# Max tiles of two neighbouring phases shared out by the number of filler matmuls in each

## The chip, the core and the metric

The kernel runs on one core of one Trainium2 chip. The core has a matrix engine (PE, whose weight loads are listed apart as PEld), a vector engine (DVE), a scalar engine for activations (ACT), a general engine (POOL) and a queue that issues transfers (SP). Each engine works through its own list of instructions in order and waits for the others on semaphores. The metric is the time of the core in device microseconds (us), lower is better; a kernel is run several times and the median counts.

## What is computed

The inputs are a matrix `x` of 2048 tokens by 640 channels and weights. The output mixes two branches with a gate per token.

```python
def _A_ref(x, wq, wk, wv, wo):          # 32 heads of 20 channels, one shared k and v
    q = (x @ wq).reshape(B, S, H, Dh).transpose(0, 2, 1, 3)
    k = x @ wk
    v = x @ wv
    scores = jnp.einsum("bhqd,bkd->bhqk", q, k) * (Dh ** -0.5)
    p = softmax(scores)
    o = jnp.einsum("bhqk,bkd->bhqd", p, v)
    return o.transpose(0, 2, 1, 3).reshape(B, S, H * Dh) @ wo

def _B_ref(x, w1, b1, w2, b2):          # an MLP over the token axis
    h = layernorm(x)
    u = gelu(jnp.einsum("bsd,sf->bdf", h, w1) + b1)     # F = 1728
    return (jnp.einsum("bdf,fs->bds", u, w2) + b2).transpose(0, 2, 1)

g = sigmoid((x * gate_w).sum(-1, keepdims=True))
out = g * _A_ref(...) + (1 - g) * _B_ref(...)
```

All is float32. Where a product needs the accuracy, the kernel splits a factor in a high and a low part and adds three products.

## The kernel before

**Stages.** A first stage (L147 to L380) projects `q`, `k`, `v` and normalizes `x`. A second stage (L499 to L532) does the first 10 of 28 groups of the MLP's first layer. Then comes the main loop (L906), 513 passes long, with which the change deals. A short piece (L943 to L957) ends the kernel.

**A phase.** One pass `k` of the main loop is called a phase here. Its number modulo 2 is `b`. The matrix engine is used as two row halves of 64 rows each, which stream side by side: half 0 has rows 0 to 63, half 1 has rows 64 to 127. In phase `k`, half `b` is the own half and half `1-b` is the filler half. A phase issues four kinds of matmuls:

- *Scores* (`qk`, L568): four matmuls of 62 x 512 on the own half, two for unit `k-1` and two for unit `k`. Each writes a bank of the pool `ps_s` (three buffers), and ACT turns it into `p` with an exponential (L578).
- *Max tiles* (`ms_next`, L398): matmuls of 60 x 512 on either half. They form the same scores ahead of time, only to find each row's maximum. Each writes a bank of the pool `ps_m` (three buffers) at L410, and DVE reduces it to one number per row (L413). There are 2048 of them. Within a pair of phases four are taken on each half.
- *Fillers*: matmuls of 64 x 320 on the filler half, which do the MLP's first layer (L828), its second layer (L668) or the output projection (L776), by the stage. They add up in one bank, `ps_g` (one buffer). Since the two halves take turns in adding to that bank, `signal` (L586) lets DVE write a small `flag` (L588) after the last filler of a phase, and the first filler of the next phase waits for that flag (`other_tile`, L581).
- *The product with v* (`pv_mm`, L596): at the end of each phase, with all 128 rows and in column tiles of 32. It adds unit `k-1` to the output `o`. Its four pieces need four `p` tiles, two of them from this phase's first two scores.

**The order in a phase.** L910 to L920 write the order out by hand. `lane_x` (L891) puts the own half's scores and max tiles in turns, a max tile first while there are any. `lane_f` (L898) puts the fillers of the other half, then `signal`, then that half's max tiles. `beside` (L880) merges the two lists by their running times, with `X_US` = 0.232 for a score or max tile and `F_US` = 0.147 for a filler (L878). It keeps the last item of the own half until the other list is empty:

```python
            if k == x and len(lanes[k]) == 1 and lanes[1 - k]:
                k = 1 - k
```

The result is one list for the matrix engine, and the reduces stand on DVE's list in the order of their max tiles, with `flag` where `signal` fell.

**How many fillers.** `batches` (L837) cuts each group of fillers into phases, and `ph` (L873) holds them. By its integer division the pairs of an even and the next odd phase have these fillers:

- first layer of the MLP, 90 pairs: 36 with (9, 9) and 54 with (10, 10);
- between the layers, 2 pairs with (0, 0), phases 180 to 183;
- second layer, 128 pairs, in turns (9, 10), (10, 11), (10, 10), (10, 11), phases 184 to 439;
- output projection, 24 pairs: 8 with (7, 7), 8 with (8, 8) in turns, phases 440 to 471, then 8 with (15, 15), phases 472 to 487;
- phase 488 (`k_tail`, L851) and after: no max tiles are left, and their fillers come from another list.

L910 gives the max tiles: three to the own half and one to the filler half where a phase has fewer than 12 fillers, else four and none.

**Work of DVE beside the max tiles.** Once in 16 phases `pv_mm` finishes an output group: DVE transposes it (L611), takes a reciprocal (L614) and, two phases later, transposes back (L618). These stand behind the reduces of the phase after which they are issued. The back transpose is issued after phases whose number is 3 modulo 16.

Of the kernel before, what the change touches and what calls it, by code (L numbers as in the profile page):

```python
# [37 lines left out]
def mix_kernel(ctx: ExitStack, tc: tile.TileContext, A_x, A_wq, A_wk, A_wv, A_wo,  # L38
               B_x, B_w1, B_b1, B_w2, B_b2, gate_w, out):
    nc = tc.nc  # L40
    x = A_x[0]
# [94 lines left out]
    def new_qmax(n):  # L136
        if n < NU and n not in qmax:
            qmax[n] = load_q(n, "qmx")
# [259 lines left out]
    def ms_next(b):  # L398
        k = given[b]
        if k >= 32 * NU:  # L400
            return None
        given[b] += 1
        n, r = divmod(k, 32)
        (kq, pr), qt = divmod(r // 4, 2), r % 4

        def step():
            if n not in mtiles:
                mtiles[n] = mpool.tile([P, 16, 4], F32, name="mp")
            ms = ps_m.tile([P, NB], F32, name="ms")
            nc.tensor.matmul(ms, qmax[n][64 * b:64 * b + 60, pr, qt * P:(qt + 1) * P],  # L410
                             kst[64 * b:64 * b + 60, kq * NB:(kq + 1) * NB], start=True, stop=True)
            c = (2 * b + pr) * 4 + qt
            nc.vector.tensor_reduce(mtiles[n][:, c, kq:kq + 1], ms, axis=AX.X, op=ALU.max)  # L413
            issued[b] += 1
            if min(issued) == 32 * n + 1:
                new_qmax(n + 1)

        return step

    def ms_done():  # L420
        n = len(row_max)
        if n < NU and min(issued) >= 32 * (n + 1):
            mm = mmpool.tile([P, 16], F32, name="mm")
            nc.vector.tensor_reduce(mm, mtiles.pop(n), axis=AX.X, op=ALU.max)
            mn = mmpool.tile([P, 2, 16], F32R, name="mn")
            nc.gpsimd.tensor_scalar(mm, mm, -1.0, None, op0=ALU.mult)
            nc.gpsimd.tensor_copy(mn[:, 0, :], mm)
            nc.gpsimd.tensor_sub(mn[:, 1, :], mm, f32(mn[:, 0, :]))
            row_max[n] = mn

    def store_max(n):
        mn = row_max[n]
        mt = mpool.tile([P, 32], F32, name="mt")
        nc.vector.transpose(mt, f32(mn).rearrange("p j c -> p (j c)"))
        nc.sync.dma_start(out=m_scr[n], in_=mt)

    def fetch_max(n):
        src = m_scr[n].rearrange("(i j b r) e -> j b r i e", j=2, b=2, r=8)
        for b in range(2):
            for j in range(2):  # L440
                rows = f32(qtiles[n][64 * b + 60 + j:64 * b + 61 + j])
                nc.sync.dma_start(out=rows.rearrange("o p (t i e) -> o (p t) i e", i=4, e=32), in_=src[j, b][None])
# [51 lines left out]
    def pop_chain():  # L494
        f = chain.pop(0) if chain else None
        if f:
            f()
# [70 lines left out]
    def qk(u, pr, b):  # L568
        n, kb = units[u]
        if kb == 4 and pr == 0 and b == 0:  # L570
            new_q(n + 1)
        q = qtiles[n]
        odd_s[0] ^= 1
        s = ps_m.tile([P, NB], F32, name="ms") if spare[0] and odd_s[0] and not loaded else ps_s.tile([P, NB], F32, name="s")
        nc.tensor.matmul(s, kst[64 * b:64 * b + 62, kb * P:(kb + 1) * P], q[64 * b:64 * b + 62, pr, :],  # L575
                         start=True, stop=True)
        p = pp_pool.tile([P, NB], F32, name="p")
        nc.scalar.activation(p, s, AF.Exp, scale=SCALE)  # L578
        ptiles[u, 2 * pr + b] = p
# [127 lines left out]
    def tail_load(i):  # L707
        if i < len(jobs):
            st, r0, r1 = jobs[i]
            cols = slice(st * P, (st + 1) * P)  # L710
            oT, yt = room(i)
            c0, c1 = r0 // P, r1 // P
            for j in range(2):
                nc.sync.dma_start(out=f32(oT[:, j, c0:c1]),
                                  in_=o_scr[j, r0:c1 * P, cols].rearrange("(c p) s -> p c s", p=P))
                if r1 > c1 * P:
                    nc.sync.dma_start(out=f32(oT[:r1 - c1 * P, j, c1]), in_=o_scr[j, c1 * P:r1, cols])
            if r0 == 0:
                nc.sync.dma_start(out=yt, in_=y_scr[cols, :])
            loaded.append(i)  # L720
# [31 lines left out]
    def tail_take(h, n):  # L752
        out = []
        while len(out) < n and tail[h] and tail[h][0][0] in loaded:
            out.append(tail[h].pop(0)[1])
        return out
# [43 lines left out]
    def last_wo():  # L800
        raw = fin.tile([P, D], F32, name="yo")
        nc.gpsimd.memset(raw, 0.0)
        for hh in range(4):
            r = (H - 4 + hh) * DH
            nc.sync.dma_start(out=raw[32 * hh:32 * hh + DH, :], in_=A_wo[r:r + DH, :])
        return raw

    def split_last(raw):
        hi, lo = spare_row(0, F32R), spare_row(1, F32R)
        nc.gpsimd.tensor_copy(hi, raw)  # L810
        nc.gpsimd.tensor_sub(lo, raw, f32(hi))
        return hi, lo
# [38 lines left out]
    k_tail = len(units) - TAIL  # L851
    todo = [divmod(i, FC) for i in range(PRO, 2 * FC)]
    seq = batches([b1_jobs(*t) for t in todo], [5] * len(todo))
    for i, (steps, rest, done) in enumerate(seq):
        item, j = divmod(i + 1, 5)
# [17 lines left out]
    ph = [(rows[1 - b], rest if b else [], done if b else []) for rows, rest, done in seq for b in range(2)]  # L873
# [3 lines left out]

    X_US, F_US = 0.232, 0.147  # L878

    def beside(rows0, rows64, x):  # L880
        lanes = [list(rows0), list(rows64)]
        at = [0.0, 0.0]
        while lanes[0] or lanes[1]:
            k = 0 if lanes[0] and (not lanes[1] or at[0] <= at[1]) else 1
            if k == x and len(lanes[k]) == 1 and lanes[1 - k]:
                k = 1 - k
            us, f = lanes[k].pop(0)
            f()
            at[k] += us

    def lane_x(ss, ms):  # L891
        out = []
        for x in ss:
            out += [(X_US, y) for y in ms[:1]] + [(X_US, x)]
            ms = ms[1:]
        return out + [(X_US, y) for y in ms]

    def lane_f(ms, fs, end):  # L898
        return [(F_US, f) for f in fs] + [(0.0, f) for f in [signal] + end] + [(X_US, y) for y in ms]
# [4 lines left out]
    with tc.manual_schedule(engines={mybir.EngineType.PE, mybir.EngineType.DVE, mybir.EngineType.Activation,  # L904
                                     mybir.EngineType.Pool, mybir.EngineType.SP}):
        for k in range(len(units) + 1):  # L906
            b = k % 2
            ss = [lambda u=u, pr=pr: qk(u, pr, b) for u in (k - 1, k) for pr in range(2) if 0 <= u < len(units)]
            fs, rest, done = ph[k] if k < k_tail else ([], [], [])
            ms = [[f for f in (ms_next(x) for _ in range(c)) if f] for x, c in (((b, 3), (1 - b, 1)) if len(fs) < 12 else ((b, 4), (1 - b, 0)))]  # L910
            lanes = [None, None]
            lanes[b] = lane_x(ss, ms[0])
            if k >= k_tail:
                rate = [len(t) / max(1, len(units) - k) for t in tail]
                own = tail_take(b, max(0, math.ceil(rate[b] - 2 * X_US / F_US)))
                lanes[b] = [x for i, y in enumerate(lanes[b])
                            for x in [y] + [(F_US, f) for f in own[len(own) * i // len(lanes[b]):len(own) * (i + 1) // len(lanes[b])]]]
                fs = tail_take(1 - b, math.ceil(rate[1 - b] + 2 * X_US / F_US))
            lanes[1 - b] = lane_f(ms[1], fs, done)
            beside(*lanes, b)  # L920
            ms_done()
            spare[0] = len(row_max) == NU
            for _ in range(2 if spare[0] else 1):
                f = later.pop(0) if later else None
                if f:
                    f()
            pop_chain()
            for f in rest:
                f()
            if k == k_tail - 4:  # L930
                raw = last_wo()
            if k == k_tail - 2:
                w_last = split_last(raw)
            if 13 <= k - k_tail < 17:
                tail_load(8 + k - k_tail - 13)
            if k:
                pv_mm(k - 1)
                n, kb = units[k - 1]
                if kb == 7 and n + 1 < NU:
                    store_max(n + 1)  # L940
                if kb == 9 and n + 1 < NU:
                    fetch_max(n + 1)
# [36 lines left out]
```

## Time and profile before

| quantity | value |
|---|---|
| median of 3 runs | 1727.07 us (1726.58 to 1728.19) |
| the profiled execution's own time | 1729.04 us |
| its span, first to last instruction | 1727.2 us |
| matrix engine busy | 1707.6 us, 99% of the span |
| DVE busy | 1450.4 us, 84% |
| ACT busy | 1187.3 us, 69% |
| POOL busy | 567.9 us, 33% |
| DMA, moved | 133.86 MB, mean 77 GB/s |
| mean granted matrix clock | 0.997 |

The profiled execution is one of its own, 1.84 us longer than its span and 1.97 us longer than the median of the other runs. Busy time of the matrix engine counts the two halves as one, so 99% does not tell that both halves are full. A row of the timeline gives the start and the length of an instruction or of several equal ones in a row (x and a number), and in brackets how long the engine had been idle before and what ended it. A weight load (PEld) that waits is the place where a matmul waits.

### The profile page before, as it was taken

The page shows a single profiled execution, that of the slowest core. Times are in us where ns is not written, and L with a number is a line of the kernel's source. Part 1 is how long each engine was busy: PE and PEld are TensorE (multiplying, and loading weights), DVE is VectorE, ACT ScalarE, POOL GpSimd, SP SyncE. Part 2 cuts the span into 40 slices and gives each one's busy share as a digit, 9 for nine tenths or more (in the row PEclk, how much of TensorE's full clock was granted, in tenths as well). Part 3 has the DMA queues.
Part 4 walks back from the last instruction along what each step waited for, and adds up shares of the span by engine and source line. Part 5 has one row for each costly group of instructions (what it writes and reads, how often), then busy time and mean ns, then how long its engine had stood idle before and what let it go on. Part 6 is the DMA issues. An engine that isn't in the chain of part 4 may idle for free.

```text
span 1727.2 us, 38831 instructions
## 1 busy us (share of the span) xinstructions
PE 1707.6 (99%) x14877; PEld 1110.6 (64%) x14877; DVE 1450.4 (84%) x2936; ACT 1187.3 (69%) x2313; POOL 567.9 (33%) x677
## 2 busy tenths in 40 slices
PE   9999999999999999999999999999999999999998
PEld 6889766666666666566666666666666666556665
DVE  6669988888888888888888888888888888888724
ACT  3434577777777777777777777777777777777764
POOL 5547644454444454332122222211222111111200
PEclk9999999999999999999999999999999999999999
DMA  6665312222222222112222222121122122244411
GB/s 200 194 162 130 103 53 59 69 58 75 63 70 69 69 63 51 47 47 68 61 68 67 58 61 61 55 57 49 46 57 61 53 61 63 74 138 131 143 52 36
DMA packets 164573, 133.86 MB, mean 77 GB/s; under 512 B 27639, under 2 KB 129428, under 8 KB 164388
## 3 DMA queue, kind: packets, MB, share of 16 engines
q1 hardware_dynamic: 164388, 131.39, 27.2%
q8 instruction: 117, 1.92, 0.5%
q14 instruction: 68, 0.56, 0.1%
HBM read 98.69 MB, written 31.65 MB: 75 GB/s over the span
## 4 chain that ended last, share of the span: by engine, by line
PE 95%; DVE 3%; DMA 1%; SPq 0%; ACT 0%; issue 0%; DVEq 0%; ACTq 0%
PE o L602 30%; PE s L575 17%; PE ms L410 17%; PE g L668 11%; PE g L828 8%; PE pp L261 4%; PE g L776 2%; PE pu L517 2%; PE ms L733 2%; DVE mp L413 2%; PE g L733 0%; DMA wr<-in_B_w_dram 0%; SPq L159 0%; DMA ht<-in_A_wq_dram 0%; PE pt L253 0%; DMA q_scr<-ql 0%
## 5 line engine op out<-in xcount | busy, mean ns | idle before, releaser
L413 DVE TENSOR_REDUCE mp<-ms 128x1 f32<-128x512 f32 x2048 | 1278.2, 684 | 173.3 <-PE ms L410 169.5
L578 ACT ACTIVATE p<-s 128x512 f32<-128x512 f32 x2048 | 1070.3, 602 | 412.0 <-PE s L575 406.2
L410 PE MATMUL ms<-kst,qmx 60*128 60x512 f32 x2048 | 847.7, 421 | 8.3 <-DVE mp L413 7.5
L575 PE MATMUL s<-qst,kst 62*128 62x512 f32 x2048 | 750.9, 403 | 0.1
L602 PE MATMUL o<-p,v_sb 128*32 128x512 f32 x4096 | 558.9, 605 | 0.5 <-ACT p L578 0.5
L410 PEld LDWEIGHTS ms<-kst,qmx 60*128 60x128 f32 x2048 | 379.0, 185 | 225.6 <-DVE flag L588 180.3
L575 PEld LDWEIGHTS s<-qst,kst 62*128 62x128 f32 x2048 | 380.8, 186 | 12.3 <-issue 10.9
L828 PE MATMUL g<-slot,wh 64*128 64x320 f32 x1152 | 281.5, 319 | 0.0
L828 PEld LDWEIGHTS g<-slot,wh 64*128 64x128 f32 x1152 | 191.0, 185 | 59.9 <-DVE flag L588 59.9
L668 PE MATMUL g<-slot,w2h 64*128 64x320 f32 x864 | 209.9, 319 | 0.0
L668 PE MATMUL g<-u,w2h 64*128 64x320 f32 x864 | 209.8, 319 | 0.0
L828 PE MATMUL g<-slot,wl 64*128 64x320 f32 x576 | 180.0, 313 | 0.0
L602 PEld LDWEIGHTS o<-p,v_sb 128*32 128x32 f32 x4096 | 93.7, 108 | 132.0 <-issue 123.3
L668 PEld LDWEIGHTS g<-slot,w2h 64*128 64x128 f32 x864 | 142.2, 184 | 53.7 <-DVE flag L588 53.7
L668 PEld LDWEIGHTS g<-u,w2h 64*128 64x128 f32 x864 | 142.2, 184 | 53.7 <-DVE flag L588 53.7
L615 POOL TENSOR_TENSOR ot<-ot,rl 128x512 f32<-128x512 f32 x30 | 31.5, 1048 | 405.1 <-DVE rl L614 396.4
L113 POOL TENSOR_TENSOR wl<-wr,wh 128x512 fp32r<-128x512 f32 x112 | 149.0, 1336 | 42.5 <-ACT wh L110 32.7
L668 PE MATMUL g<-u,w2l 64*128 64x320 f32 x432 | 133.7, 309 | 0.0
L668 PE MATMUL g<-slot,w2l 64*128 64x320 f32 x432 | 133.7, 309 | 0.0
L828 PEld LDWEIGHTS g<-slot,wl 64*128 64x128 f32 x576 | 106.7, 185 | 15.1 <-DVE flag L588 15.1
L517 PE MATMUL pu<-slot,wh 64*128 64x320 f32 x640 | 83.9, 312 | 0.0
L776 PEld LDWEIGHTS g<-slot 64*128 64x128 f32 x480 | 70.3, 184 | 20.1 <-DVE flag L588 16.8
(175 smaller groups left out, 1573.6 us busy)
## 6 DMA issues: line engine op xcount, KB each, us to landing
wr<-in_B_w_dram SPq DMA_DIRECT2D x104, 256.0 KB
qmx<-q_scr SPq DMA_DIRECT2D x192, 80.0 KB
qst<-q_scr SPq DMA_DIRECT2D x192, 80.0 KB
w2r<-in_B_w_dram SPq DMA_DIRECT2D x16, 448.0 KB
w2r<-in_B_w_dram SPq DMA_DIRECT2D x16, 384.0 KB
q_scr<-qh SPq DMA_DIRECT2D x20, 256.0 KB
q_scr<-ql SPq DMA_DIRECT2D x20, 256.0 KB
y_scr<-yo SPq DMA_DIRECT2D x16, 320.0 KB
```

Source lines behind the costliest of these rows:

```text
L113: nc.gpsimd.tensor_sub(wl, wr, f32(wh))
L261: nc.tensor.matmul(pp, w, t, start=first and n == 0, stop=not more and n == len(steps) - 1)
L410: nc.tensor.matmul(ms, qmax[n][64 * b:64 * b + 60, pr, qt * P:(qt + 1) * P], kst[64 * b:64 * b + 60, kq * NB:(kq + 1) * NB], start=True, s ...
L413: nc.vector.tensor_reduce(mtiles[n][:, c, kq:kq + 1], ms, axis=AX.X, op=ALU.max)
L517: nc.tensor.matmul(pu[r][:, :HD2], w[rows, c, :], h[rows, st, :], start=(st == 0 and k == 0), stop=(st == NS - 1 and k == 2))
L575: nc.tensor.matmul(s, kst[64 * b:64 * b + 62, kb * P:(kb + 1) * P], q[64 * b:64 * b + 62, pr, :], start=True, stop=True)
L578: nc.scalar.activation(p, s, AF.Exp, scale=SCALE)
L602: nc.tensor.matmul(o[32 * hh:32 * hh + 32, :], v_sb[:, kb, :], ptiles.pop((u, hh)), start=(kb == 0), stop=(kb == NS - 1), skip_group_check ...
L668: other_tile(half, nc.tensor.matmul(hold["p"][:, :HD2], w[r, fc % FH, :], u[d][r, fc, :], start=(hold["n"] == 1), stop=(hold["n"] == 6 * F ...
L733: nc.tensor.matmul(acc[d, h][:, :HD2], o[r, c, :], w[r, c, d * HD2:(d + 1) * HD2], start=first, stop=last)
L776: other_tile(half, nc.tensor.matmul(hold["p"][:, :HD2], o[r, c, :], w[r, c, d * HD2:(d + 1) * HD2], start=(hold["n"] == 1), stop=(hold["n" ...
L828: other_tile(half, nc.tensor.matmul(hold["p"][:, :HD2], w[r, st % HS, :], h[d][r, st, :], start=(hold["n"] == 1), stop=(hold["n"] == 6 * NS)))
```

## The change

Instead of the fixed rule (three and one, or four and none), a new function `share` looks at both phases of a pair. It tries five ways in which the filler halves of the even and the odd phase can take max tiles, (1, 1), (0, 1), (0, 0), (2, 2) and (3, 3), and takes the one whose cost is least; the own half of each phase gets four less what the other phase's filler half takes, so that both halves still have four in the pair. The cost is the longer of the two lists by `X_US` and `F_US`, added over both phases.

```diff
     X_US, F_US = 0.232, 0.147
 
+    def share(k):
+        n = [len(ph[j][0]) if j < k_tail else 0 for j in (k & ~1, k | 1)]
+
+        def cost(c):
+            return sum(max((4 + 4 - c[1 - i]) * X_US, n[i] * F_US + c[i] * X_US) for i in range(2))
+
+        c = min(((1, 1), (0, 1), (0, 0), (2, 2), (3, 3)), key=cost)
+        return 4 - c[1 - k % 2], c[k % 2]
+
     def beside(rows0, rows64, x):
...
-            ms = [[f for f in (ms_next(x) for _ in range(c)) if f] for x, c in (((b, 3), (1 - b, 1)) if len(fs) < 12 else ((b, 4), (1 - b, 0)))]
+            ms = [[f for f in (ms_next(x) for _ in range(c)) if f] for x, c in zip((b, 1 - b), share(k))]
```

With the fillers above, three kinds of pairs come out otherwise than before. In the 64 pairs with (10, 11) fillers the even phase has three max tiles on its own half and none on its filler half (before: three and one), and the odd phase has four and one (before: three and one). In the 8 pairs with (7, 7) both phases have two and two. In the 2 pairs with (0, 0) both have one and three. All other pairs, and the number of instructions of every kind, are as before; DVE, ACT, POOL and SP get the same work, the reduces in their new order.

## The prediction

> **What bounds the kernel now.** I read the page first: the engines, the chain that ended last, the costliest groups.
>
> ```profile
> span 1727.2 us, 38831 instructions
> ...
> PE 95%; DVE 3%; DMA 1%; SPq 0%; ACT 0%; issue 0%; DVEq 0%; ACTq 0%
> ...
> L413 DVE TENSOR_REDUCE mp<-ms 128x1 f32<-128x512 f32 x2048 | 1278.2, 684 | 173.3 <-PE ms L410 169.5
> ```
>
> The chain lies on the matrix engine for 95% of the span, so a phase's length is what its list there takes. But DVE's reduces of the 2048 max tiles alone are 1278 us, and nearly all of them fall into 488 phases of about 3 us. A change in when max tiles come must be checked against DVE. So I went to the timeline of the matrix engine for one pair with (10, 11) fillers, phases 226 and 227, the kind that changes most often.
>
> ```profile
> 856.50 0.49 PE L410 MATMUL ms<-kst,qmx 60*128 60x512 f32 x1
> ...
> 858.07 0.39 PE L410 MATMUL ms<-kst,qmx 60*128 60x512 f32 x1
> 858.39 1.07 PE L602 MATMUL o<-p,v_sb 128*32 128x512 f32 x8
> 859.39 0.41 PE L668 MATMUL g<-slot,w2h 64*128 64x320 f32 x1
> 859.40 0.50 PE L410 MATMUL ms<-kst,qmx 60*128 60x512 f32 x1
> ...
> 859.73 0.39 PE L575 MATMUL s<-qst,kst 62*128 62x512 f32 x1
> ...
> 860.21 0.39 PE L575 MATMUL s<-qst,kst 62*128 62x512 f32 x1
> ...
> 860.44 0.39 PE L410 MATMUL ms<-kst,qmx 60*128 60x512 f32 x1
> ...
> 860.90 0.47 PE L575 MATMUL s<-qst,kst 62*128 62x512 f32 x1
> ...
> 861.10 0.39 PE L410 MATMUL ms<-kst,qmx 60*128 60x512 f32 x1
> 861.42 1.06 PE L602 MATMUL o<-p,v_sb 128*32 128x512 f32 x8
> 862.42 0.50 PE L410 MATMUL ms<-kst,qmx 60*128 60x512 f32 x1
> ```
>
> The even phase runs from 856.50 to 859.39, 2.89 us; the odd one from 859.39 to 862.42, 3.03. Each ends with the product with v (L602), 1.00 from its start to the next phase. It begins 0.32 after the last max tile of the filler half (858.07 to 858.39, 861.10 to 861.42): both phases end by the filler half, as the cost function holds. In a running list a score or max tile takes 0.23 (860.21 to 860.44), at a cold start 0.33 (859.40 to 859.73), since the weight load is not hidden then. DVE in the same two phases, and at the start of the next:
>
> ```profile
> 859.93 2.50 DVE L413 TENSOR_REDUCE mp<-ms 128x1 f32<-128x512 f32 x4 [0.24 <-PE ms L410]
> 861.76 0.06 DVE L588 MEMSET flag<- 1x1 f32 x1
> 862.34 0.70 DVE L618 STREAM_TRANSPOSE on<-ot 128x512 f32<-128x512 f32 x1
> 862.97 2.48 DVE L413 TENSOR_REDUCE mp<-ms 128x1 f32<-128x512 f32 x4
> ```
>
> The first reduce starts 0.54 after the phase (859.39 to 859.93); they follow each other every (2.50 - 0.68)/3 = 0.61. So a phase's tiles leave their banks at about 1.22, 1.83 and 2.43 after its start. DVE works off one tile of the phase before during the product with v, which costs nobody time.
>
> **The change part by part.** By the kernel's own constants it should gain: a (10, 11) pair goes from 1.702 + 1.849 = 3.551 to 1.624 + 1.856 = 3.480, 0.071 less; a (7, 7) pair from 3.248 to 2.986; a (0, 0) pair from 3.248 to 2.320. With 64, 8 and 2 pairs that is 4.5 + 2.1 + 1.9 = 8.5 us. The constants know neither DVE nor ACT.
>
> *The odd phases of the 64 pairs.* They now issue five max tiles, four on the own half and one after the last filler. The pool has three banks, so the fourth tile waits for the first one's reduce and the fifth for the second one's. How such a wait looks today is seen in a phase with 7 fillers, where the fourth tile comes early:
>
> ```profile
> 1498.82 2.50 DVE L413 TENSOR_REDUCE mp<-ms 128x1 f32<-128x512 f32 x4 [0.44 <-PE ms L410]
> ...
> 1499.56 0.18 PEld L410 LDWEIGHTS ms<-kst,qmx 60*128 60x128 f32 x1 [0.25 <-DVE mp L413]
> ...
> 1499.57 0.73 PE L575 MATMUL s<-qst,kst 62*128 62x512 f32 x2
> 1500.23 1.06 PE L602 MATMUL o<-p,v_sb 128*32 128x512 f32 x8
> ```
>
> The first reduce started at 1498.82 and lasts 0.68; the weight load that waited for it starts at 1499.56, 0.06 after its end. From there to the product with v it is 0.67, with two scores on the own half behind the load. With one matmul on each half, as in the changed odd phase, it is 0.67 - 0.23 = 0.44. Four own tiles in one phase exist already, with 15 fillers:
>
> ```profile
> 1591.33 0.50 PE L410 MATMUL ms<-kst,qmx 60*128 60x512 f32 x1
> ...
> 1593.07 0.48 PE L575 MATMUL s<-qst,kst 62*128 62x512 f32 x1
> ```
>
> ```profile
> 1591.86 2.48 DVE L413 TENSOR_REDUCE mp<-ms 128x1 f32<-128x512 f32 x4 [0.90 <-PE ms L410]
> 1594.29 0.06 DVE L588 MEMSET flag<- 1x1 f32 x1
> ```
>
> There DVE reduces from 0.53 after the start, the last score of eight stands at 1.74, and the flag comes at 2.96, after four reduces. So in the changed odd phase the fifth tile's load can start at 0.54 + 0.61 + 0.68 + 0.06 = 1.88. It would have run at 861.10 - 859.39 = 1.71. Behind it stand the own half's last score and the product with v, which thus starts at 1.88 + 0.44 = 2.32 instead of 2.03. I take 0.28 for the difference, as every summand is rounded: 64 x 0.28 = +17.9 us. The bounds: without any wait the row of eight would set the end, at 1.74 + 0.34 = 2.08, +0.05 or +3.2 us in all (0.34 is an estimate of the way from the last score to the product, from the 0.32 of a max tile); with a further 0.06 of release time +21.8 us. The flag at 2.96 + 0.06 does not bind, since the next phase starts at 2.32 + 1.00 = 3.32.
>
> *The even phases of these pairs* lose the filler half's tile. Their end would go from 858.07 + 0.32 to the own half's seven matmuls, about 0.04 earlier. But the product's second half needs the exponential of the second score:
>
> ```profile
> 857.27 2.06 ACT L578 ACTIVATE p<-s 128x512 f32<-128x512 f32 x4 [0.82 <-PE s L575]
> ```
>
> Four exponentials in 2.06, each 0.60, follow every 0.49; the second ends at 857.27 + 0.49 + 0.60 = 858.36, 0.03 before the product starts today. So ACT gives back most of the 0.04. A phase with the same seven and only 8 fillers shows it, the one from 1516.27 here:
>
> ```profile
> 1510.02 0.49 PE L410 MATMUL ms<-kst,qmx 60*128 60x512 f32 x1
> ...
> 1516.27 0.50 PE L410 MATMUL ms<-kst,qmx 60*128 60x512 f32 x1
> ...
> 1519.16 0.50 PE L410 MATMUL ms<-kst,qmx 60*128 60x512 f32 x1
> ```
>
> It lasts 2.89, as today's even phase with 10. I take -0.3 us for all 64, between -2.6 (0.04 each) and 0.
>
> *The back transpose* comes after 16 of these odd phases. There the fifth reduce now stands from 2.96 to 3.57, the next phase starts at 3.32, so the transpose runs from 0.25 into it and the first reduce follows 0.63 later (862.34 to 862.97), at 0.88 instead of 0.55. That next phase has (10, 10), and its fourth tile waits for this reduce: 0.88 + 0.68 + 0.06 = 1.62, and the product starts 0.44 later, at 2.06 instead of 1.89. Between 0.10 and 0.17, I take 0.13: 16 x 0.13 = +2.1 us.
>
> *The 8 pairs with (7, 7)* get the waiting fourth tile out of the way of the scores. A phase then cannot fall below the 2.89 that the exponentials leave. Two of the pairs are long today (1510.02 to 1516.27, 6.25 us for two phases against 2 x 2.89 or a little more); the others are at 2.9 to 3.0 a phase. I take -0.8 us, between -1.9 (2 x 0.47 and 16 x 0.06) and 0.
>
> *The 2 pairs with (0, 0)*, one phase today:
>
> ```profile
> 723.38 0.50 PE L410 MATMUL ms<-kst,qmx 60*128 60x512 f32 x2
> ...
> 724.20 0.40 PE L575 MATMUL s<-qst,kst 62*128 62x512 f32 x1
> 724.67 0.18 PEld L410 LDWEIGHTS ms<-kst,qmx 60*128 60x128 f32 x1 [0.51 <-DVE mp L413]
> ...
> 725.56 1.06 PE L602 MATMUL o<-p,v_sb 128*32 128x512 f32 x8
> ```
>
> The fourth tile waits until 1.29 after the start for the first reduce, before and after. In the even phases two scores stand behind it instead of a tile and two scores: -0.22. In the odd ones the built order puts three scores behind it, so the second score comes at about 1.39 instead of 0.82; its exponential ends 0.57 later, at 2.43 instead of 1.86, and the product, at 2.18 today, waits for it: about +0.28. Together +0.1 us, between -0.9 and +1.1.
>
> Sum: 17.9 - 0.3 + 2.1 - 0.8 + 0.1 = +19.0 us on the profiled span of 1727.2. The profiled execution lies 1.97 above the median of the other runs; I put the difference on the median: 1727.07 + 19.0 = 1746.1 us.
>
> **The rivals.**
>
> *The held tile's weights are loaded while it waits.* Then the tile and the score start at 1.88 without the cold start's 0.10 (0.33 - 0.23): 80 x 0.10 = 8 us less, 1738. Against it stands the wait on the weight load itself, at 1499.56. The Trainium skill, "TensorE: Matmul & The Clock Gate", section on the array of 16 sub-arrays, says that this engine's queue can pull weight loads ahead of matmuls in flight. By that rule the sum would be this rival's 1738; the row at 1499.56 speaks against it for a load that carries the wait. 8%.
>
> *The fifth tile does not wait*, because its bank is free sooner than I hold. Then +3.2 - 0.3 - 0.8 = +2.1, 1729.2, no change that can be told. For it: DVE has three reduces in the even phase and is done early. Against it: the bank belongs to this phase's own second tile, which cannot be reduced before 1.13. 7%.
>
> *The constants hold*, and the change does what it was reckoned to: -8.5, 1718.6, faster. The even phases would have to drop by 0.078 each. Against it: the 8-filler phase, with an even shorter filler list, lasts 2.89. 4%.
>
> *DVE's lateness carries over* into all 64 following even phases, as it does behind the back transpose: 48 more x 0.13 = +6.2, 1752. It decides once the fifth reduce ends after the next phase's first tile is ready, that is after 3.32 + 0.54 = 3.86; I have 3.57, so 0.29 would have to go. 8%.
>
> **How the numbers follow.** My forecast, 1746, has 73%. Its own range is 1742 to 1750. The first rival and the last widen that to 1737 (a little below the first, whose summands are rounded too) and 1752, which holds 81% or a little more. This kernel's measurement can tell about 0.2% (3.5 us) from no change: faster is the third rival alone, 4%; the same is the second, 7%; slower is the rest, 89%.
>
> **What would show it.** The table of waits has one row for this:
>
> ```profile
> PEld ms L410 <- DVE mp L413: 42.8, 63, 3.6
> ```
>
> It should gain about 64 + 16 waits of 0.2 to 0.3 us, to some 140 times and 60 us. In a changed odd phase the fifth max tile's load should stand about 1.88 after the start, held by the reduce, the product with v at 2.32 and the phase at 3.31; the even phase stays at 2.89. Wrong would be a fifth tile at 1.71 with the product at 2.08 (then the second rival holds), a product at 2.21 (the first), an even phase near 2.81 (the third), or first reduces later than 0.6 after the start in even phases other than those behind the back transpose (the last).

## The result, and the profile after

The changed kernel takes 1746.97 us (median of 4 runs, 1742.81 to 1748.13) against 1727.63 us for the kernel before (4 runs, 1726.58 to 1728.82). The ratio is 1.0107 with a 95% interval of 1.0089 to 1.0126: it is slower by 1.1%. Its profiled execution took 1746.17 us. The page of the changed kernel, the lines that answer to those of before:

```profile
span 1744.4 us, 38845 instructions
...
PE 95%; DVE 3%; DMA 1%; SPq 0%; ACT 0%; issue 0%; ACTq 0%; DVEq 0%
...
L413 DVE TENSOR_REDUCE mp<-ms 128x1 f32<-128x512 f32 x2048 | 1276.7, 683 | 194.6 <-PE ms L410 189.1
```

Nothing here says where the time went: the chain lies on the matrix engine as before, the reduces take what they took, and DVE is idle 21 us longer in front of them (194.6 against 173.3). The 14 instructions more (38831 before) are semaphore instructions on DVE's list; the matmuls, weight loads, reduces and exponentials are as many as before. The place shows in the timeline. The matrix engine's rows of phases 226 and 227, the same pair as before the change (start, length, instruction):

```profile
857.45 0.49 PE L410 MATMUL ms<-kst,qmx 60*128 60x512 f32 x1
...
858.97 0.39 PE L575 MATMUL s<-qst,kst 62*128 62x512 f32 x1
859.30 1.12 PE L602 MATMUL o<-p,v_sb 128*32 128x512 f32 x8
860.35 0.50 PE L410 MATMUL ms<-kst,qmx 60*128 60x512 f32 x1
...
861.86 0.40 PE L410 MATMUL ms<-kst,qmx 60*128 60x512 f32 x1
862.23 0.50 PE L410 MATMUL ms<-kst,qmx 60*128 60x512 f32 x1
862.23 0.49 PE L575 MATMUL s<-qst,kst 62*128 62x512 f32 x1
862.66 1.06 PE L602 MATMUL o<-p,v_sb 128*32 128x512 f32 x8
863.65 0.50 PE L410 MATMUL ms<-kst,qmx 60*128 60x512 f32 x1
```

The even phase lasts 860.35 - 857.45 = 2.90 us, as before. The odd one lasts 3.30, where it was 3.03. Its fifth max tile starts 862.23 - 860.35 = 1.88 after the phase's start, not at 1.71, together with the last score, and the product with v follows at 2.31 instead of 2.03. The weight loads of that moment, with what ended the wait in brackets, and DVE's rows:

```profile
862.22 0.18 PEld L410 LDWEIGHTS ms<-kst,qmx 60*128 60x128 f32 x1 [0.28 <-DVE mp L413]
862.23 0.18 PEld L575 LDWEIGHTS s<-qst,kst 62*128 62x128 f32 x1
```

```profile
860.88 3.10 DVE L413 TENSOR_REDUCE mp<-ms 128x1 f32<-128x512 f32 x5 [0.84 <-PE ms L410]
863.31 0.06 DVE L588 MEMSET flag<- 1x1 f32 x1
863.89 0.70 DVE L618 STREAM_TRANSPOSE on<-ot 128x512 f32<-128x512 f32 x1
864.52 2.47 DVE L413 TENSOR_REDUCE mp<-ms 128x1 f32<-128x512 f32 x4
```

The load is released by a reduce, the phase's second. Five reduces run without a break from 0.53 after the phase's start; in front of them DVE was idle for 0.84 us, through part of the product with v and the odd phase's first max tile, since no finished max tile stood ready. Before the change it was idle for 0.24 there, as it still had the even phase's fourth reduce to do. That is the exchange: the even phase leaves DVE without work, the odd one gives it five tiles at once, and three banks hold three.

For a balance of the whole loop I took every phase from the start of its first matmul to that of the next phase, phases 2 to 510, in both traces, and averaged by kind:

| phases | number | before, us | after, us | difference, us in all | forecast |
|---|---|---|---|---|---|
| (10, 11), odd | 64 | 3.028 | 3.303 | +17.6 | +17.9 |
| (10, 11), even | 64 | 2.895 | 2.891 | -0.3 | -0.3 |
| behind a back transpose | 16 | 2.892 | 3.007 | +1.8 | +2.1 |
| (7, 7) | 16 | 2.996 | 2.938 | -0.9 | -0.8 |
| (0, 0), even and odd | 2 + 2 | 3.196, 3.171 | 2.965, 3.478 | +0.15 | +0.1 |
| all of the loop | 509 | | | +18.5 | +19.0 |

The spans differ by 17.2 only, since the loop's phase 2 begins at 199.4 us in this execution and at 201.6 in that of before, while what follows phase 510 takes 0.8 us longer. That start lies before anything the change touches; over the profiles of seven kernels with whole reduces it falls between 198.9 and 202.5.

### The profile page after: what moved, and what is told of

It is laid out like the page before. It is cut to its first block, busy times and chain, and to the rows that moved or that the text cites. A ratio compares the mean times of both kernels' runs of the same rounds, so it can differ in the third digit from the quotient of the medians.

```text
span 1744.4 us, 38845 instructions
## 1 busy us (share of the span) xinstructions
PE 1725.5 (99%) x14877; PEld 1119.2 (64%) x14877; DVE 1447.4 (83%) x2936; ACT 1189.9 (68%) x2313; POOL 569.1 (33%) x677
## 4 chain that ended last, share of the span: by engine, by line
PE 95%; DVE 3%; DMA 1%; SPq 0%; ACT 0%; issue 0%; ACTq 0%; DVEq 0%
PE o L602 30%; PE ms L410 18%; PE s L575 16%; PE g L668 11%; PE g L828 8%; PE pp L261 4%; PE g L776 2%; PE pu L517 2%; PE ms L733 2%; DVE mp L413 1%; PE g L733 0%; PE ms L963 0%; DMA ht<-in_A_wq_dram 0%; SPq L159 0%; DMA q_scr<-ql 0%; DMA wr<-in_B_w_dram 0%
## 5 line engine op out<-in xcount | busy, mean ns | idle before, releaser
L413 DVE TENSOR_REDUCE mp<-ms 128x1 f32<-128x512 f32 x2048 | 1276.7, 683 | 194.6 <-PE ms L410 189.1
L575 PE MATMUL s<-qst,kst 62*128 62x512 f32 x2048 | 765.4, 405 | 0.1
L602 PEld LDWEIGHTS o<-p,v_sb 128*32 128x32 f32 x4096 | 97.4, 108 | 126.0 <-issue 117.7
```

The source lines that it names most:

```text
L602: nc.tensor.matmul(o[32 * hh:32 * hh + 32, :], v_sb[:, kb, :], ptiles.pop((u, hh)), start=(kb == 0), stop=(kb == NS - 1), skip_group_check ...
```

## The experiments

In all of them phases are measured as in the table above, and means are over all phases of a kind.

**Only the pairs with (7, 7), and only the pairs with (10, 11).** Two kernels divide the change:

```diff
-        c = min(((1, 1), (0, 1), (0, 0), (2, 2), (3, 3)), key=cost)
+        c = {(7, 7): (2, 2), (15, 15): (0, 0)}.get(tuple(n), (1, 1))     # first kernel
+        c = {(10, 11): (0, 1), (15, 15): (0, 0)}.get(tuple(n), (1, 1))   # second kernel
```

> Only the 8 pairs with (7, 7) fillers are shared out anew (two and two); all other pairs have the max tiles of the kernel before. My theory puts the whole loss on the odd phases of the 64 (10, 11) pairs: here the (10, 11) pairs stay at 2.89 and 3.03 us, the (7, 7) phases go to 2.93 and 2.95 as in the changed kernel, and the time is that of the kernel before less 0.9 us (the sum over the 16 phases in the changed kernel), so a ratio of 0.9995, which cannot be told from 1. Rival: the loss lies in the new order as such, wherever it stands; then the (7, 7) phases cost too and the time is above the kernel before.

> Only the 64 pairs with (10, 11) fillers are shared out anew (three and none, then four and one). My theory: the odd phases last 3.30 us instead of 3.03 (64 x 0.275 = 17.6), the 16 phases behind a back transpose 3.01 instead of 2.89 (1.8), the even ones 2.89 as before: 19.2 us more than the kernel before, ratio 1.011, the full loss of the change and a little more. Rival: part of the loss is due to the other 10 pairs; then clearly less than 19 us.

The first took 1728.52 us against 1729.1 for the kernel before beside it, ratio 0.9996 (0.9987 to 1.0006): no change that can be told. One of its (7, 7) pairs, the matrix engine's rows at the start of the even phase, the odd one and the next:

```profile
1499.02 0.50 PE L410 MATMUL ms<-kst,qmx 60*128 60x512 f32 x1
...
1501.95 0.50 PE L410 MATMUL ms<-kst,qmx 60*128 60x512 f32 x1
...
1504.90 0.50 PE L410 MATMUL ms<-kst,qmx 60*128 60x512 f32 x1
```

They last 2.93 and 2.95; over all 16 phases the gain is 0.9 us, and the (10, 11) phases stay at 2.895 and 3.031. The second kernel took 1745.98 us, ratio 1.0097 (1.0080 to 1.0114). Its odd (10, 11) phases last 3.305, the ones behind a back transpose 3.005, and all other kinds are as before; its loop is 19.6 us longer, against 19.2 expected. So the loss is that of the 64 pairs, and the other ten have no part in it.

**Short reduces, in the changed kernel and in the one before.** This is the test of the cause: the same matmuls in the same order, with DVE needing less time for each tile. Both kernels leave out half of the keys in the row maximum.

```diff
-            nc.vector.tensor_reduce(mtiles[n][:, c, kq:kq + 1], ms, axis=AX.X, op=ALU.max)
+            nc.vector.tensor_reduce(mtiles[n][:, c, kq:kq + 1], ms[:, :NB // 2], axis=AX.X, op=ALU.max)
```

> The changed kernel, with each max tile reduced over its first 256 of 512 columns, so that the row maximum is taken over half of the keys; the matmuls stay whole. My theory, that the fifth max tile of an odd (10, 11) phase waits for the second tile's reduce: with a reduce of some 0.35 us instead of 0.60 the bank is free before the fifth tile's turn at 1.71, no wait is left, the row of eight ends the phase with the product at 2.08, the phase lasts 3.08, and against the kernel before with the same short reduces it is 64 x 0.05 = 3.2 us longer, 2 to 4 in all. The phases behind a back transpose are back at 2.89. Rival: the odd phase is long because eight matmuls stand on one half and one cold behind the fillers on the other, whatever DVE does: then it stays at 3.30 and the difference at 18 us.

> The kernel before, with each max tile reduced over its first 256 of 512 columns, so that the row maximum is taken over half of the keys. It is the base for the changed kernel with short reduces. My theory: no bank wait was on the path of its (10, 11) phases, so these stay at 2.89 and 3.03 us, and only the phases with 0 and 7 fillers, where a fourth tile waits today, get shorter (four and sixteen of them, by 0.05 to 0.3 each): 1 to 2 us less than the kernel before, ratio 0.999. Rival: DVE sets the pace of the loop in general; then all phases shrink and the time falls by tens of us.

Measured: 1724.29 us with the change and 1721.63 without, 2.7 us apart (ratios to the kernel before 0.9966, 0.9951 to 0.9980, and 0.9954, 0.9939 to 0.9969); the loops differ by 2.0 us. The odd phase 227 of the changed kernel with short reduces, matrix engine and DVE:

```profile
855.63 0.50 PE L410 MATMUL ms<-kst,qmx 60*128 60x512 f32 x1
...
857.13 0.39 PE L410 MATMUL ms<-kst,qmx 60*128 60x512 f32 x1
857.34 0.39 PE L410 MATMUL ms<-kst,qmx 60*128 60x512 f32 x1
857.37 0.39 PE L575 MATMUL s<-qst,kst 62*128 62x512 f32 x1
857.68 1.06 PE L602 MATMUL o<-p,v_sb 128*32 128x512 f32 x8
858.68 0.50 PE L410 MATMUL ms<-kst,qmx 60*128 60x512 f32 x1
```

```profile
851.78 0.42 DVE L413 TENSOR_REDUCE mp<-ms 128x1 f32<-128x256 f32 x1
...
856.16 2.17 DVE L413 TENSOR_REDUCE mp<-ms 128x1 f32<-128x256 f32 x5 [1.35 <-PE ms L410]
```

A reduce now takes 0.42 us. The fifth tile runs at 1.71, its old place, the last score at 1.74 and the product at 2.05: the row of eight ends the phase. The mean of the 64 is 3.061 against 3.032 in the kernel before with short reduces, so 0.03 of the 0.275 is the row of eight and the rest is the wait for DVE, with the cold start behind it. The phases behind a back transpose are at 2.888.

The kernel before with short reduces is 0.46% faster than the kernel before, and I had expected 0.1%. Its loop is as expected, 1.5 us shorter: 2.0 less in the phases with 0 and 7 fillers, and 0.5 more, scattered, in the others. The rest lies ahead of the loop: phase 2 begins at 195.7 us. One stretch of the second stage, with the busy time of the matrix engine, weight loads, DVE, ACT and POOL and the number of instructions; the first row is of the kernel before, the second of the one with short reduces:

```profile
140.00:170.00 30.00, 28.75 (x359) 27.76 (x361) 27.90 (x50) 13.82 (x28) 20.59 (x17) 1.00 0.47 125
```

```profile
140.00:170.00 30.00, 30.00 (x391) 30.00 (x390) 23.27 (x52) 14.53 (x28) 20.33 (x18) 1.00 0.58 144
```

There DVE is busy for 27.90 of 30 us, and with short reduces the matrix engine gets 391 matmuls done instead of 359. How much of the 5.8 us at the start is that and how much its scatter is open; in the changed kernel with short reduces phase 2 begins at 197.9.

**Four and none in both phases of the (10, 11) pairs.** The line stands in place of the changed kernel's `c = min(...)`, here and in the next experiment; all other pairs are as in the kernel before.

```diff
+        c = {(10, 11): (0, 0), (15, 15): (0, 0)}.get(tuple(n), (1, 1))
```

> The 64 (10, 11) pairs get four max tiles on the own half and none on the filler half in both phases; all else as in the kernel before. There is no fifth tile, but eight matmuls stand on the own half of both phases. My theory: no max tile waits for a bank, the product starts at 1.74 + 0.34 = 2.08 and both phases last 3.08 us, 6.16 a pair against 5.92 before: 64 x 0.24 = 15.2 us more, ratio 1.009; the flag, ready at about 3.06, is just in time. Rivals: the constants give 3.712 against 3.551, 64 x 0.161 = 10.3 us more; or four own tiles make DVE late as such, and the phases go beyond 3.2 each, 20 us and more.

1744.31 us against 1727.34, ratio 1.0099 (1.0082 to 1.0116). Matrix engine, the odd phase:

```profile
859.65 0.50 PE L410 MATMUL ms<-kst,qmx 60*128 60x512 f32 x1
...
861.40 0.40 PE L575 MATMUL s<-qst,kst 62*128 62x512 f32 x1
861.73 1.06 PE L602 MATMUL o<-p,v_sb 128*32 128x512 f32 x8
862.73 0.50 PE L410 MATMUL ms<-kst,qmx 60*128 60x512 f32 x1
```

The last score stands at 1.75, the product at 2.08, the phase lasts 3.08. The means are 3.097 (even) and 3.072 (odd), 6.17 a pair against the 6.16 expected. The loop is 16.6 us longer where 15.2 were expected: the pairs give 15.8, and phases with (10, 10) another 0.7. So a row of eight costs about 3.08 in either phase, and no max tile in these phases shows a wait for a reduce. After the even ones the next phase starts 1.03 instead of 1.00 behind the product; its first load comes 0.07 after the end of the flag, which may be what holds it. By the kernel's constants this order costs 0.16 us a pair more than the one before; the runs show 0.25.

**The fifth tile in the even phase.**

```diff
+        c = {(10, 11): (1, 0), (15, 15): (0, 0)}.get(tuple(n), (1, 1))
```

> The 64 (10, 11) pairs the other way round: the even phase has four max tiles on its own half and one on its filler half, the odd phase three and none; all else as in the kernel before. By the constants of the kernel this costs the same as the change, 3.480 a pair. My theory: five tiles in one phase wait wherever they stand. The even phase then lasts 3.31 instead of 2.89 (fifth tile's load at 1.88, product at 2.31), the odd one 2.95 instead of 3.03 (three own tiles, held by the exponential): 64 x (0.42 - 0.08) = 21 us more than before, ratio 1.012. Rival: the fifth tile does not matter, the row of eight does: then the even phase lasts 3.08 and the sum is 64 x (0.19 - 0.08) = 7 us.

1748.47 us, ratio 1.0122 (1.0107 to 1.0137). The starts of the two phases and of the next one, with the held load and the product between:

```profile
859.17 0.50 PE L410 MATMUL ms<-kst,qmx 60*128 60x512 f32 x1
...
861.48 1.06 PE L602 MATMUL o<-p,v_sb 128*32 128x512 f32 x8
862.48 0.49 PE L410 MATMUL ms<-kst,qmx 60*128 60x512 f32 x1
...
865.42 0.50 PE L410 MATMUL ms<-kst,qmx 60*128 60x512 f32 x1
```

```profile
861.05 0.18 PEld L410 LDWEIGHTS ms<-kst,qmx 60*128 60x128 f32 x1 [0.40 <-DVE mp L413]
```

Again the load is held until 1.88 and the product comes at 2.31. The even phases have a mean of 3.303, the odd ones 2.946, and the loop is 21.5 us longer, 21 expected. Five max tiles in one phase cost the same 3.30 wherever they stand, whether the phase has 10 or 11 fillers.

**The back transpose one phase later**, on top of the change.

```diff
-            later.extend((None, scale, back, high, low))
+            later.extend((None, scale, None, back, high, low))
```

> The changed kernel with the back transpose and the two steps behind it issued one phase later, after a phase with four max tiles instead of five. My theory: the 16 phases whose number is 4 modulo 16 fall from 3.01 to 2.89 us, as DVE has only the fifth reduce to finish there, the next ones (5 modulo 16) stay at 2.95, and 1.8 us of the loss go, which the time of one run cannot tell. The odd (10, 11) phases stay at 3.30. Rival: the fifth reduce alone makes these phases late; then they stay at 3.01.

One run, 1746.78 us. The starts of the phases 228, 229 and 230, and DVE's transpose:

```profile
866.45 0.50 PE L410 MATMUL ms<-kst,qmx 60*128 60x512 f32 x1
...
869.34 0.50 PE L410 MATMUL ms<-kst,qmx 60*128 60x512 f32 x1
...
872.28 0.50 PE L410 MATMUL ms<-kst,qmx 60*128 60x512 f32 x1
```

```profile
869.40 0.70 DVE L618 STREAM_TRANSPOSE on<-ot 128x512 f32<-128x512 f32 x1
```

The empty steps that this leaves in `later` are skipped at the loop's end. The phase that had been 3.01 lasts 2.89, the next, which now has the transpose at its start, 2.94; the loop is 1.9 us shorter than the changed kernel's. So those 16 phases were late by the transpose behind the fifth reduce, not by the fifth reduce alone.

Apart from the two with short reduces, which do not compute the whole maximum, none of these beats the kernel before. The best, the change for the (7, 7) pairs alone, cannot be told from it.

## Why the prediction was right

The median came out at 1746.97 us against 1746.1. That agreement to 1 us is partly luck: the loop's start alone scatters by 3.6 us between the profiles above, and the median of the kernel before moved too (1727.07 to 1727.63). What the forecast can be held to is the loop, 18.5 us against 19.0, and the rows behind it.

- *The odd phases.* The forecast had the fifth tile's load at 1.88, the product at 2.32 (with 0.28 taken for the difference) and the flag not in the way. Its summands as written add up to 1.89, so that the product would stand at 2.33, 0.30 late; they are rounded, and the smaller 0.28 was a choice that the trace bears out. The trace has 1.88, 2.31 and +0.275 on the mean, and no phase waits for the flag: the next one starts 1.00 after the product, as before. That DVE's reduce is the cause is shown by the short reduces, which bring the tile back to 1.71; that it is five tiles in a phase is shown by the kernel with the fifth in the even phase.
- *The even phases.* They were to give back what they gain, to the exponential. In the changed kernel the product starts at 859.30 - 857.45 = 1.85 instead of 1.89, and the next phase starts 1.05 after it instead of 1.00. ACT's row in that phase:

```profile
858.22 2.06 ACT L578 ACTIVATE p<-s 128x512 f32<-128x512 f32 x4 [0.82 <-PE s L575]
```

  The second exponential ends at 858.22 + 0.49 + 0.60 = 859.31, with the product already under way: its first two pieces start at 859.30, the other two only at 859.36, where before the change all four started within 0.03. So the 0.04 was not to be had here.
- *The back transpose* cost 0.115 a phase where 0.13 was taken, within its bounds. The fourth tile's load comes at 1.57 or 1.58 after the phase's start where 1.62 was reckoned.
- *The (7, 7) pairs* gave 0.9 where 0.8 was taken. They do not reach the 2.89 named as their floor: the next phase starts 1.09 (even) and 1.04 (odd) after the product, where it was 1.00.
- *The (0, 0) pairs* came out as a gain and a loss of nearly one size. An odd phase of the changed kernel, matrix engine, ACT and one weight load of the product:

```profile
720.95 0.72 PE L410 MATMUL ms<-kst,qmx 60*128 60x512 f32 x3
721.28 0.39 PE L575 MATMUL s<-qst,kst 62*128 62x512 f32 x1
722.22 0.50 PE L410 MATMUL ms<-kst,qmx 60*128 60x512 f32 x1 [0.55 <-DVE mp L413]
722.23 0.96 PE L575 MATMUL s<-qst,kst 62*128 62x512 f32 x3
723.12 1.37 PE L602 MATMUL o<-p,v_sb 128*32 128x512 f32 x8
724.42 0.50 PE L410 MATMUL ms<-kst,qmx 60*128 60x512 f32 x2
```

```profile
721.74 0.60 ACT L578 ACTIVATE p<-s 128x512 f32<-128x512 f32 x1 [0.79 <-PE s L575]
722.80 1.58 ACT L578 ACTIVATE p<-s 128x512 f32<-128x512 f32 x3 [0.46 <-PE ms L410]
```

```profile
723.45 0.14 PEld L602 LDWEIGHTS o<-p,v_sb 128*32 128x32 f32 x2 [0.17 <-ACT p L578]
```

  Three scores stand behind the held tile, ACT gets its second one at 722.80, 1.85 after the start, and the product starts at its old place (2.17), but a weight load within it waits for that exponential, and the product is stretched from 1.06 to 1.37 us.
- *The rivals.* A held tile whose weights are loaded meanwhile would have brought the product to 2.21; it stands at 2.31, 0.43 after the held load, so the cold start is paid. The load of the last score, which waits for nothing of DVE's and goes to the other half, starts only 0.01 after the held one. Both matmuls are 0.50 and 0.49 long in their rows, against 0.40 in a running list: both loads were cold. The rule of the Trainium skill, "TensorE: Matmul & The Clock Gate", section on the array of 16 sub-arrays, that the queue can pull weight loads ahead of matmuls in flight, did not help here: neither load was pulled ahead of the wait. That DVE's lateness would spread to all following phases is out, as those not behind a transpose stay as they were (2.89 with (10, 10), 2.93 with (9, 10)). That the constants hold is out too: the even phases stay at 2.89 and the time rose.
- *What was off* is one of the signs named, not a term of the sum. The row of waits of a max tile's load for a reduce was to grow to some 140 times and 60 us:

```profile
PEld ms L410 <- DVE mp L413: 40.7, 97, 2.5
```

  It has more entries (97 against 63) but less time in all (42.8 before). Taken apart by phases, 64 entries with 17.4 us are the fifth tiles of the odd phases, as forecast. The 16 loads behind a back transpose waited for only 0.11 us each and do not appear. The rest of the row shrank: loads at the start of a phase, idle for 0.84 us through the product with v, whose release is put now under a max tile's reduce and now under the flag, went from 29 to 11 (24.3 to 9.2 us), and waits in (7, 7) phases from 16 to 4 (4.6 to 0.9 us). The sum of the row was thus no sign to go by; the single load in the timeline is.

## What to carry to other kernels

A cost function that balances two lists of one engine is blind to the engine that empties the buffers behind it: count how many items a stretch hands over at once, against the buffers and against the consumer's time for one. A producer of evenly spaced items may look unbalanced on its own engine and still be the better order. Before shortening a list, look for the next thing that holds its end, here an exponential that needs only 0.03 us less than the list, and for a phase in the same trace that already has the new length.

## What the runs showed of the hardware that was not expected

A wait on a semaphore at a weight load cost more than the wait. The fifth tile was 0.17 late (1.71 to 1.88), but the product that follows was 0.28 late, because that tile's load and the load of the next matmul on the other half both began only then and were not hidden. In a running list a matmul of 512 columns takes 0.23 (860.21 to 860.44 before the change); behind the load held at 1499.56 in the kernel before, the two scores start 0.34 apart. Behind the wait stood the phase's last matmuls, so nothing could make up for it. The forecast took this from one row of the kernel before; in the changed kernel it holds for all 64 odd phases, with the load at 1.88 and the product between 2.30 and 2.31 after the start.
